# k and v of the first eight units on 128 partitions; five w_out tiles in own memory, decoded among the units

## The chip, the cores and the metric

The program runs on one core of a Trainium2 chip. The metric is the time of one execution in microseconds on the device; a kernel's time is the median of its runs. The kernel before took 1453.11 us (three runs, 1452.28 to 1455.67).

## The reference

q, k, v, p and the output are fp32, and three parts follow one another. `w_in`, `w_out` and the weights of the last part come as 8-byte numbers, so a tile of 128 x 512 is 512 KB.

```
# q, k, v: (8 batches, 8 heads, 576 tokens, 64);  p: (8, 8, 32, 64)
p_packed = sm_attn(p, k, v)            # softmax(p k^T / 8) v : 32 rows per head
out = sm_attn(q, p_packed, p_packed)   # every q row attends to those 32 rows
x = out.transpose(0, 2, 1, 3).reshape(4608, 512)
r = relu(x @ w_in)                     # w_in 512 x 2048
x = (s * r * r + b) @ w_out            # w_out 2048 x 512
y = ((x @ w1) * (x @ w2)) @ w3 @ w_out2   # 512 -> 1024 -> 1024 -> 512
```

A softmax over 576 keys does not care in which order the keys stand, as long as scores, exponentials and the rows of v use the same order.

## The kernel before, in words

A *unit* is half the heads (four) of one batch; there are 16, and `N1 = 8` of them, batches 0 to 3, are worked off in a loop of its own at the start (`for i in range(N1 + OFF)`, line 584, eleven passes, i = 0 to 10). The other eight are planned into the later steps and keep their old form. In the loop several units are under way at once: pass i transposes k of unit i, takes the scores of unit i - 1, transposes the exponentials of unit i - 2 and multiplies unit i - 3 by v.

The steps of a unit, with their names and lines:

- `load_k`, `load_v` (lines 281 and 290): one DMA each, 576 KB, three buffers each. Token `6 p + j` of a head stands on partition `p` of 96, so a partition holds four heads of six tokens of 64 numbers; one run in memory is six tokens, 1536 bytes.
- `A_tr(u, h)` (line 324): head h of k is transposed on TensorE, two tokens' worth of columns (128) at a time, three transposes of 96 columns, and copied out by ScalarE (288 columns). Ahead of them stand multiplications of zeros (`zero`), three for units 0 to 4 and one after, whose result is overwritten.
- `B_s1` (line 341): scores, eight matmuls of 288 columns. The contraction is over 64 rows (one of two parities of token) and four heads stand side by side as 4 x 32 columns of the array. `B_sm1`, `B_sm2`: maximum on DVE, exponential on ScalarE, reciprocal.
- `C_tr(u, hf)` (line 393): two times three transposes of 96 columns of the exponentials, each with one copy by ScalarE.
- `D_mm` (line 406): 6 x 4 matmuls, 96 rows of contraction, 32 x 64 results. `D_ev` transposes the result and stores it in `ppT`.

Between these the loop decodes the 16 tiles of w_in (`decode_win`: a raw 8-byte tile is turned into fp32 by one ScalarE square, lines 141 and 142, and four DVE operations, lines 146 to 165), works on q of batch 0 (`q_step`), and from pass `WS = 6` to 9 multiplies the results of batches 0 and 1 by w_in (`w_pair`). The decoded w_in lies in eight tiles with the tag `sh` (`winx`), and `win_store` writes it to memory for later use. All fp32 matmuls that aren't transposes appear as two records in the trace.

After the loop come 256 steps, 32 for each of eight batches (16 tiles of w_out on each half of the tokens): `step_h` (line 679, six matmuls of 288 columns, then relu and square) runs three steps ahead of `step_x` (line 710, twelve matmuls with one w_out tile, `wo_t[f]`). The first 16 steps need the 16 w_out tiles as they come: `wo_load` fetches a raw tile, `wo_dec` (line 511) decodes it and splits it into two parts (`split`, line 76: ScalarE the upper, DVE the rest). Raw tiles of w_in, w_out and later weights share four buffers (`RAWB`), decoded ones three (`XB`); the later loads of the stored w_in (`W_load`) take these three too. w_out tiles 0 to 7 lie in a pool `wop` that is opened once the unit loop's pools are closed, tiles 8 to 15 take over the eight `sh` tiles.

Order: the lines stand in program order, but the framework moves instructions by its own simulated time, except those pinned by `keep_in_program_order`, among them nearly all loads on SP, the queue that issues all DMAs. Each engine then works strictly in order.

Of the kernel before, what the change touches and what calls it, by code (L numbers as in the profile page):

```python
# [9 lines left out]
F32 = mybir.dt.float32  # L10
F32R = mybir.dt.float32r
# [4 lines left out]
AF = mybir.ActivationFunctionType  # L16
# [6 lines left out]
def fused_kernel(  # L23
# [144 lines left out]
    if True:  # L168
# [97 lines left out]
        def kt_ps(name):  # L266
            return ps0.tile([P, 512], F32, tag="kt", name=name, bufs=2)
# [4 lines left out]
        def m_ps(name):  # L272
            return ps0.tile([P, 512], F32, tag="m", name=name, bufs=2)
# [3 lines left out]
            for n in range(NFC * NPAIR // 2)  # L277
        ]
        kt, vt, kT, S1, E1, E1T, PV = {}, {}, {}, {}, {}, {}, {}

        def load_k(u):
            b, g = divmod(u, NG)
            kt[u] = a1.tile([TP, 4, NJ, D], F32, tag="k", name="k", bufs=3)
            ins = nc.sync.dma_start(
                out=kt[u], in_=k[b, 4 * g:4 * g + 4].rearrange("h (p j) d -> p h j d", j=NJ)
            )
            if u:
                tc.keep_in_program_order(ins)

        def load_v(u):  # L290
            b, g = divmod(u, NG)
            vt[u] = a1.tile([TP, 4, NJ, D], F32, tag="v", name="v", bufs=3)
            ins = nc.sync.dma_start(
                out=vt[u], in_=v[b, 4 * g:4 * g + 4].rearrange("h (p j) d -> p h j d", j=NJ)
            )
            tc.keep_in_program_order(ins)

        pTd, pz = {}, {}
        A = {"p": a1}
# [23 lines left out]

        def A_tr(u, h):

            if h == 0:
                kT[u] = A["p"].tile([P, 4, HS], F32, tag="kT", name="kT", bufs=2 if u < N1 else 1)
            ps = kt_ps("ktp") if u < N1 else a2_ps("ktp")
            src = kt[u][:, h] if u < N1 else kt.pop((u, h))
            if u < N1:  # L330
                for _ in range(3 if u < 5 else 1):
                    nc.tensor.matmul(ps, zero[:, :P], zero, start=True, stop=True)
            for jj in range(HJ):
                nc.tensor.transpose(
                    ps[:, jj * TP:(jj + 1) * TP],
                    src[:, 2 * jj:2 * jj + 2, :].rearrange("p j d -> p (j d)"),
                    ident[:TP, :TP],
                )
            nc.scalar.copy(kT[u][:, h], ps[:, :HS])

        def B_s1(u):
            if u < N1:
                t = ps0.tile([P, 2, 512], F32, tag="s1", name="s1p")
                ps = t[:, 0], t[:, 1], t
            else:
                ps = a2_ps("s1p"), a2_ps("s1p")
            for par in range(2):
                rows = slice(D * par, D * (par + 1))
                for h in range(4):
                    nc.tensor.matmul(  # L350
                        ps[par][NP * h:NP * (h + 1), :HS], pTd[u // 4][rows, u % 4, NP * h:NP * (h + 1)],
                        kT[u][rows, h], start=True, stop=True,
                    )
            S1[u] = ps

        def B_sm1(u):
            ps = S1.pop(u)[2]
            mx = a1.tile([P, 4], F32, tag="mx", name="mx", bufs=3)
            nc.vector.tensor_reduce(out=mx[:, 0:1], in_=ps[:, :, :HS], axis=AX.XY, op=ALU.max)
            nc.vector.tensor_scalar_mul(mx[:, 1:2], mx[:, 0:1], -SC)  # L360
            e = a1.tile([P, 2, HS], F32, tag="E1", name="E1", bufs=2)
            nc.scalar.activation(
                e, ps[:, :, :HS], AF.Exp, bias=mx[:, 1:2], scale=SC, accum_out=mx[:, 2:3]
            )
            E1[u] = (e, mx)

# [24 lines left out]
            rec[u] = r  # L391

        def C_tr(u, hf):
            if hf == 0:
                E1T[u] = A["p"].tile([TP, NJ, P], F32, tag="E1T", name="E1T", bufs=2 if u < N1 else 1)
            ps = m_ps("etp") if u < N1 else a2_ps("etp")
            for jj in range(HJ):
                nc.tensor.transpose(
                    ps[:TP, jj * P:(jj + 1) * P], E1[u][0][:, hf, jj * TP:(jj + 1) * TP], ident
                )  # L400
            dst = E1T[u][:, hf * HJ:(hf + 1) * HJ, :].rearrange("p a b -> p (a b)")
            nc.scalar.copy(dst, ps[:TP, :HJ * P])
# [3 lines left out]
        def D_mm(u):  # L406

            ps = m_ps("pvp") if u < N1 else a2_ps("pvp")  # L410
            for j in range(NJ):
                for h in range(4):
                    nc.tensor.matmul(
                        ps[NP * h:NP * (h + 1), :D], E1T[u][:, j, NP * h:NP * (h + 1)],
                        vt[u][:, h, 2 * (j % HJ) + j // HJ, :], start=j == 0, stop=j == NJ - 1,
                    )
            x = A["p"].tile([P, 2, D], F32, tag="pvx", name="pvx", bufs=2 if u < N1 else 1)
            nc.vector.tensor_tensor(
                out=x, in0=ps[:, None, :D].to_broadcast([P, 2, D]),
                in1=rec.pop(u).to_broadcast([P, 2, D]), op=ALU.mult,  # L420
            )
            PVX[u] = x
# [88 lines left out]
        def wo_dec(f):  # L511
            d = wod.pop(f)
            d.square()
            d.bits1()
            d.bits2()
            if f >= NW // 2:
                wo_t[f] = sh.tile([P, 2, DM], F32R, tag="sh", name=f"wo{f}", bufs=NW // 2)
            else:
                wo_t[f] = wop[0].tile([P, 2, DM], F32R, name=f"wo{f}")
            split(wo_t[f][:, 0, :], wo_t[f][:, 1, :], d.f)  # L520

        NW = NFC * NPAIR
        OFF = 3

        NWARM = 18
        zero = wch_p.tile([P, 2, FC], F32, tag="wpst", name="zero", bufs=4)[:, 0]
# [53 lines left out]
        def w_pair(j):  # L580
            wps = q_ps if j % 2 == 0 else kt_ps
            W_pair(j, [wps("wps") for _ in range(2)])

        for i in range(N1 + OFF):
            jq = i - AS
            if 1 <= i < N1 + 1:
                load_v(i - 1)
            if i < N1:
                A_tr(i, 0)
            if i + 2 < N1:  # L590
                load_k(i + 2)
# [12 lines left out]
            if i >= OFF:  # L604
                D_mm(i - OFF)
            if i < N1:
                A_tr(i, 2)
            decode_win()
            if i < N1:
                A_tr(i, 3)  # L610
# [12 lines left out]
            if WS <= i < WS + 4:  # L623
                w_pair(2 * (i - WS) + 1)
            if 2 <= i < 2 + NTILE:
                load_q(0, i - 2)
            if i == N1:
                for f in range(4):
                    wo_load(f)
            if i > N1:  # L630
                for _ in range(3):
                    win_store()
        ps = ps0.tile([P, 2, 512], F32, tag="s1", name="warm")[:, 0]
        for n in range(8):
            wh = wch[0, 0][0][:, 0]
            tc.keep_in_program_order(nc.tensor.matmul(ps, wh[:, :P], wh, start=True, stop=True))
        ctx0.close()
        ctx1.close()
        wop[0] = ctx_a.enter_context(pool("wop", "right"))
        for f in range(3):  # L640
            wo_load(f + 4)
            wo_dec(f)


        ctx2 = ExitStack()
# [3 lines left out]
        def a2_ps(name):  # L649
            return psh.tile([P, 512], F32, tag="a2", name=name, bufs=2)  # L650
# [305 lines left out]
                      w3T[m, half][:, 1].rearrange("p a b -> p (a b)"), ps, pin=pin)  # L956
        for idx in range(NST):
            n, r = divmod(idx, 2 * FB1)
            if idx + 7 < FB1:
                wo_load(idx + 7)  # L960
            for _ in range(2):
                if stores:
                    win_store()
            if idx + 3 < FB1:
                wo_dec(idx + 3)
            if idx in PPS:
                pp_split(PPS.index(idx) + 1)
            if idx == PPS[2]:
# [423 lines left out]
```

## Time and profile before

| | |
|---|---|
| median of three runs | 1453.11 us |
| the profiled execution | 1454.21 us |
| its span, first to last instruction | 1451.7 us |
| mean granted TensorE clock | 0.992 of full |
| TensorE busy | 1422.3 us, 98% |
| DVE busy | 939.2 us, 65% |
| ScalarE busy | 753.1 us, 52% |
| HBM read, written | 182.98 MB, 44.04 MB |

PE is TensorE, ACT ScalarE, POOL GpSimd; SP issues the DMAs. A matmul's record is longer than the distance to the next, since matmuls overlap; the chain of waits counts only the time up to the next piece, and so shows their pace. The chain follows the work that ended last back from the end, at each step to what released it. The share of DMA is the mean over 16 engines that move the data; a little above 1 means that all were at work all the time.

### The profile page before, as it was taken

The page shows a single profiled execution, that of the slowest core. Times are in us where ns is not written, and L with a number is a line of the kernel's source. Part 1 is how long each engine was busy: PE and PEld are TensorE (multiplying, and loading weights), DVE is VectorE, ACT ScalarE, POOL GpSimd, SP SyncE. Part 2 cuts the span into 40 slices and gives each one's busy share as a digit, 9 for nine tenths or more (in the row PEclk, how much of TensorE's full clock was granted, in tenths as well). Part 3 has the DMA queues.
Part 4 walks back from the last instruction along what each step waited for, and adds up shares of the span by engine and source line. Part 5 has one row for each costly group of instructions (what it writes and reads, how often), then busy time and mean ns, then how long its engine had stood idle before and what let it go on. Part 6 is the DMA issues. An engine that isn't in the chain of part 4 may idle for free.

```text
span 1451.7 us, 28061 instructions
## 1 busy us (share of the span) xinstructions
PE 1422.3 (98%) x10858; PEld 1336.3 (92%) x10858; DVE 939.2 (65%) x1842; ACT 753.1 (52%) x1625; POOL 3.8 (0%) x38
## 2 busy tenths in 40 slices
PE   8999999999999999999999999999999999999997
PEld 5559999999999989999899998999999999999997
DVE  5769644565665776667898637466585756757556
ACT  3567655675656776567876634242243333324323
POOL 0000000000000000000000000000000000000000
PEclk8999999999999999999999999999999999999999
DMA  9967422132263344255563533776675856757551
GB/s 237 245 201 242 140 62 53 44 104 71 90 183 109 114 140 126 64 165 160 177 207 130 175 110 133 227 226 193 189 234 162 253 171 195 227 165 215 160 165 44
DMA packets 179365, 228.86 MB, mean 158 GB/s; under 512 B 55329, under 2 KB 115745, under 8 KB 179233
## 3 DMA queue, kind: packets, MB, share of 16 engines
q1 hardware_dynamic: 179232, 227.07, 53.6%
q8 instruction: 86, 1.41, 0.4%
q14 instruction: 47, 0.38, 0.1%
HBM read 182.98 MB, written 44.04 MB: 156 GB/s over the span
## 4 chain that ended last, share of the span: by engine, by line
PE 90%; ACT 3%; DMA 3%; DVE 2%; issue 1%; SPq 0%; POOL 0%; ACTq 0%; POOLq 0%; DVEq 0%
PE xps L86 9%; PE xps L90 9%; PE xps L89 9%; PE prod L86 7%; PE prod L90 7%; PE prod L89 7%; PE hps L86 5%; PE hps L90 4%; PE hps L89 4%; PE yps L89 4%; PE yps L90 4%; PE yps L86 4%; DMA raw<-in_moe_w_in_dram 2%; PE scp L204 2%; PE s1p L350 1%; PE qtp L190 1%
## 5 line engine op out<-in xcount | busy, mean ns | idle before, releaser
L90 PE MATMUL xps<-gh,wo 128*128 128x288 f32 (+1 forms) x1024 | 302.4, 299 | 0.0
L89 PE MATMUL xps<-gl,wo 128*128 128x288 f32 (+1 forms) x1024 | 302.2, 298 | 0.0
L86 PE MATMUL xps<-gh,wo 128*128 128x288 f32 (+1 forms) x1024 | 291.9, 300 | 1.6 <-DVE wo L81 1.6
L86 PE MATMUL prod<-xc,whl 128*128 128x384 f32 x672 | 226.2, 337 | 2.9 <-ACT Ta L1032 1.8
L90 PE MATMUL prod<-xc,whl 128*128 128x384 f32 x672 | 225.0, 335 | 0.0
L89 PE MATMUL prod<-xc,whl 128*128 128x384 f32 x672 | 224.8, 335 | 0.0
L89 PEld LDWEIGHTS xps<-gl,wo 128*128 128x128 f32 x1024 | 193.2, 189 | 3.0 <-issue 1.4
L90 PEld LDWEIGHTS xps<-gh,wo 128*128 128x128 f32 x1024 | 193.0, 189 | 2.8 <-issue 1.9
L86 PEld LDWEIGHTS xps<-gh,wo 128*128 128x128 f32 x1024 | 188.3, 189 | 5.0 <-POOL gh L695 2.0
L691 ACT ACTIVATE r<-hps 128x288 f32<-128x288 f32 x256 | 104.6, 410 | 134.1 <-PE hps L90 130.4
L703 DVE TENSOR_TENSOR gl<-r,gh 128x288 fp32r<-128x288 f32 x256 | 115.3, 454 | 77.5 <-ACT r L700 74.7
L86 PE MATMUL hps<-ATh,wpl 128*128 128x288 f32 x512 | 153.8, 301 | 5.9 <-ACT r L691 5.0
L1032 ACT COPY Ta<-prod 128x384 f32<-128x384 f32 x96 | 46.1, 480 | 215.4 <-PE prod L90 214.6
L90 PE MATMUL hps<-ATh,wph 128*128 128x288 f32 x512 | 152.8, 298 | 0.0
L89 PE MATMUL hps<-ATl,wph 128*128 128x288 f32 x512 | 152.6, 298 | 0.0
L90 PE MATMUL yps<-w4c,op 128*128 128x256 f32 x504 | 142.2, 282 | 0.0
L89 PE MATMUL yps<-w4c,op 128*128 128x256 f32 x504 | 142.1, 282 | 0.0
L86 PE MATMUL yps<-w4c,op 128*128 128x256 f32 x504 | 140.9, 280 | 0.0
L86 PEld LDWEIGHTS prod<-xc,whl 128*128 128x128 f32 x672 | 126.2, 188 | 7.4 <-ACT Ta L1032 3.8
L89 PEld LDWEIGHTS prod<-xc,whl 128*128 128x128 f32 x672 | 126.2, 188 | 0.0
L90 PEld LDWEIGHTS prod<-xc,whl 128*128 128x128 f32 x672 | 126.1, 188 | 0.0
L700 ACT ACTIVATE r<-r 128x288 f32<-128x288 f32 x256 | 112.7, 444 | 4.7
(158 smaller groups left out, 2582.9 us busy)
## 6 DMA issues: line engine op xcount, KB each, us to landing
whl<-whl SPq DMA_DIRECT2D x336, 256.0 KB, 3.1
raw<-in_moe_w_dram SPq DMA_DIRECT2D x32, 512.0 KB, 4.2
raw<-in_moe_w_out_dram SPq DMA_DIRECT2D x24, 512.0 KB, 4.5
x<-win SPq DMA_DIRECT2D x48, 256.0 KB, 2.8
v<-in_v_dram SPq DMA_DIRECT2D x16, 576.0 KB, 7.7
q<-in_q_dram SPq DMA_DIRECT2D x72, 128.0 KB, 4.4
x<-xst SPq DMA_DIRECT2D x16, 576.0 KB, 3.2
out_dram<-O SPq DMA_DIRECT2D x72, 128.0 KB, 2.4
```

The source lines that it names most:

```text
L86: ins = nc.tensor.matmul(ps, wl, xh, start=start, stop=False, **kw)
L89: nc.tensor.matmul(ps, wh, xl, start=False, stop=False, **kw)
L90: nc.tensor.matmul(ps, wh, xh, start=False, stop=stop, **kw)
L190: nc.tensor.transpose(ps[:, pr * P:pr * P + n], src[:n, 2 * pr:2 * pr + 2, :].rearrange("p h d -> p (h d)"), ident[:n, :n],)
L204: nc.tensor.matmul(ps[sl, c:c + 64], qT[b, t][:, pr, sl], ppT[:, b // 2, pr, b % 2, :], start=True, stop=True,)
L350: nc.tensor.matmul(ps[par][NP * h:NP * (h + 1), :HS], pTd[u // 4][rows, u % 4, NP * h:NP * (h + 1)], kT[u][rows, h], start=True, stop=True,)
L691: nc.scalar.activation(r, ps[:, :HS], AF.Relu)
L700: nc.scalar.activation(r, r, AF.Square)
L703: nc.vector.tensor_tensor(out=gl[:, :HS], in0=r, in1=gh[:, :HS].bitcast(F32), op=ALU.subtract)
L1032: tc.keep_in_program_order(nc.scalar.copy(out, src))
```

## The change

Units 0 to 7 hold their k and v differently. Two heads lie on one another on 128 partitions, 64 each, with nine tokens on a partition (one run of memory: 2304 bytes); a unit takes two DMAs for k and two for v. `A_tr` is called three times a unit instead of four, each with three transposes of 128 columns and one copy of 384; the zero matmuls ahead of them are three for units 0 to 2, two for units 3 and 4, none after. The scores are eight matmuls again, of 320 and 256 columns, laid side by side so that their 576 columns are contiguous. `C_tr` becomes 18 matmuls of 64 columns against the identity instead of six transposes, `D_mm` 36 matmuls of 64 rows instead of 24 of 96.

w_out tiles 0 to 4 get a pool of their own (`wop0`) that is there from the start; tiles 5 to 12 take over the `sh` tiles and 13 to 15 a pool opened after the loop. The first four are loaded at pass 5 and decoded at passes 7 to 10, where tiles 4 to 7 are loaded; all 16 `win_store` are issued at passes 6 to 9, four in each. After the loop tile 4 is decoded, and the steps decode five tiles ahead (`AHEAD`) where it was three, and load nine ahead where it was seven. The diff, without the parts that keep the old form for the later units:

```diff
+        J2, JE = S // 64, (S // 64 + 1) // 2
         def load_k(u):
-            kt[u] = a1.tile([TP, 4, NJ, D], F32, tag="k", name="k", bufs=3)
-            ins = nc.sync.dma_start(
-                out=kt[u], in_=k[b, 4 * g:4 * g + 4].rearrange("h (p j) d -> p h j d", j=NJ)
-            )
+            kt[u] = a1.tile([P, 2 * J2, D], F32, tag="k", name="k", bufs=3)
+            for a in range(2):
+                h0 = 4 * g + 2 * a
+                ins = nc.sync.dma_start(
+                    out=kt[u][:, a * J2:(a + 1) * J2].rearrange("p j d -> p (j d)"),
+                    in_=k[b, h0:h0 + 2].rearrange("h (p j) d -> (h p) (j d)", j=J2),
+                )
...
         def A_tr(u, h):
+            if u < N1:
+                if h == 0:
+                    kT[u] = a1.tile([P, J2, P], F32, tag="kT", name="kT", bufs=2)
+                ps = kt_ps("ktp")
+                for _ in range(3 if u < 3 else 2 if u < 5 else 0):
+                    nc.tensor.matmul(ps, zero[:, :P], zero, start=True, stop=True)
+                for c in range(3):
+                    j = 2 * (3 * h + c)
+                    nc.tensor.transpose(
+                        ps[:, c * P:(c + 1) * P],
+                        kt[u][:, j:j + 2, :].rearrange("p j d -> p (j d)"), ident,
+                    )
+                nc.scalar.copy(
+                    kT[u][:, 3 * h:3 * h + 3].rearrange("p a c -> p (a c)"), ps[:, :3 * P]
+                )
+                return
...
         def B_s1(u):
+            for odd_, h in ((o, h) for o in range(2) for h in range(4) if u < N1):
+                n = JE if odd_ == 0 else J2 - JE
+                s0, par = divmod(J2 * (h // 2) + odd_, 2)
+                rows = slice(D * par, D * (par + 1))
+                c0 = 512 - 64 * JE if odd_ == 0 else 0
+                nc.tensor.matmul(
+                    ps[odd_][NP * h:NP * (h + 1), c0:c0 + 64 * n],
+                    pTd[u // 4][rows, u % 4, NP * h:NP * (h + 1)],
+                    kT[u][rows, s0:s0 + n, 64 * (h % 2):64 * (h % 2 + 1)], start=True, stop=True,
+                )
...
         def C_tr(u, hf):
+            if u < N1:
...
+                for j in range(j0, j1):
+                    e0 = 64 * (j // 2 + (JE if j % 2 else 0))
+                    for r in range(2):
+                        nc.tensor.matmul(
+                            ps[64 * r:64 * (r + 1), 64 * (j - j0):64 * (j - j0 + 1)],
+                            E1[u][0][:, e0:e0 + 64],
+                            ident.rearrange("p (a r n) -> p r a n", r=2, n=NP)[:, r],
+                            start=True, stop=True,
+                        )
...
         def D_mm(u):
+            for j in range(J2 if u < N1 else 0):
+                for h in range(4):
+                    rows = slice(64 * (h % 2), 64 * (h % 2 + 1))
+                    nc.tensor.matmul(
+                        ps[NP * h:NP * (h + 1), :D], E1T[u][rows, j, h // 2, :],
+                        vt[u][rows, h // 2, j, :], start=j == 0, stop=j == J2 - 1,
+                    )
...
         def wo_dec(f):
-            if f >= NW // 2:
+            if WOA <= f < WOA + NW // 2:
                 wo_t[f] = sh.tile([P, 2, DM], F32R, tag="sh", name=f"wo{f}", bufs=NW // 2)
             else:
-                wo_t[f] = wop[0].tile([P, 2, DM], F32R, name=f"wo{f}")
+                wo_t[f] = wop[f >= WOA].tile([P, 2, DM], F32R, name=f"wo{f}")
-        OFF = 3
+        OFF, WOA, AHEAD = 3, 5, 5
+        wop[0] = ctx_a.enter_context(pool("wop0", "right"))
...
             if WS <= i < WS + 4:
                 w_pair(2 * (i - WS) + 1)
+                for _ in range(4):
+                    win_store()
-            if i == N1:
+            if i == WS - 1:
                 for f in range(4):
                     wo_load(f)
-            if i > N1:
-                for _ in range(3):
-                    win_store()
+            if i >= N1 - 1:
+                wo_dec(i - N1 + 1)
+                wo_load(i - N1 + 5)
...
-        wop[0] = ctx_a.enter_context(pool("wop", "right"))
-        for f in range(3):
+        wop[1] = ctx_a.enter_context(pool("wop1", "right"))
+        for f in range(4, AHEAD):
+            wo_dec(f)
             wo_load(f + 4)
-            wo_dec(f)
...
-            if idx + 7 < FB1:
-                wo_load(idx + 7)
-            for _ in range(2):
-                if stores:
-                    win_store()
-            if idx + 3 < FB1:
-                wo_dec(idx + 3)
+            if idx + AHEAD < FB1:
+                wo_dec(idx + AHEAD)
+            if idx + AHEAD + 4 < FB1:
+                wo_load(idx + AHEAD + 4)
```

## Rows read from the trace of the kernel before

**Rows 1.** The page: busy us, share of the span, instructions, of TensorE.

```profile
PE 1422.3 (98%) x10858; PEld 1336.3 (92%) x10858; DVE 939.2 (65%) x1842; ACT 753.1 (52%) x1625; POOL 3.8 (0%) x38
```

**Rows 2.** Busy us by stretch: engines, then TensorE clock, DMA share, GB/s.

```profile
10.00:30.00 20.00, 14.43 (x65) 8.71 (x66) 12.02 (x24) 6.59 (x15) 0.00 (x0) 0.66 1.02 262
...
50.00:68.70 18.70, 16.46 (x220) 10.57 (x220) 12.04 (x33) 9.78 (x25) 0.00 (x0) 1.00 1.09 242
68.70:103.30 34.60, 34.15 (x370) 15.74 (x367) 23.55 (x61) 23.42 (x56) 0.42 (x8) 1.00 0.81 232
103.30:159.20 55.90, 52.23 (x394) 49.94 (x394) 53.20 (x117) 43.66 (x102) 2.70 (x24) 0.97 0.66 201
159.20:840.00 680.80, 676.03 (x5660) 643.74 (x5660) 442.11 (x1067) 450.22 (x1058) 0.00 (x0) 1.00 0.40 120
```

**Rows 3.** Chain of waits, 60 to 104 us: start, us, what (x records).

```profile
53.15 13.27 DMA raw<-in_moe_w_in_dram
...
70.15 0.46 PE etp L398 x3
70.61 0.24 PE ktp L332
...
72.61 0.47 PE pvp L413 x24
...
78.15 0.62 PE scp L204 x16
...
101.89 1.85 PE warm L636 x8
```

**Rows 4.** Waits of TensorE, 103.3 to 159.2 us: total, times, longest us.

```profile
PE hps L86 <- ACT r L691: 2.0, 1, 2.0
PE xps L86 <- DVE wo L81: 1.6, 2, 1.0
```

**Rows 5.** Chain of waits, 103 to 160 us.

```profile
143.35 0.60 DVE x L152
...
146.46 0.34 DVE x L146
...
147.13 0.61 DVE wo L81
147.76 3.09 DMA x<-win
150.87 0.62 ACT sh L78
...
155.99 0.24 PE xps L89
156.23 0.14 PE xps L90
```

**Rows 6.** DMA of 22:26, 82:86, 1044:1048 us; counts under each size are cumulative.

```profile
DMA packets 577, 1.01 MB, mean 254 GB/s; under 512 B 28, under 2 KB 510, under 8 KB 577
...
q1 hardware_dynamic: 577, 1.01, 102.8%
...
DMA packets 403, 1.44 MB, mean 360 GB/s; under 512 B 47, under 2 KB 56, under 8 KB 402
...
q1 hardware_dynamic: 402, 1.43, 102.5%
...
DMA packets 741, 1.36 MB, mean 340 GB/s; under 512 B 78, under 2 KB 78, under 8 KB 741
...
q1 hardware_dynamic: 741, 1.36, 94.4%
```

**Rows 7.** Groups of TensorE, 0 to 110 us: busy us, mean ns, idle before.

```profile
L413 PE MATMUL pvp<-v,E1T 96*32 96x64 f32 x384 | 11.3, 224 | 0.0
```

**Rows 8.** Timeline of SP: start, us, what.

```profile
76.69 0.32 SPq L293 DMA_DIRECT2D v<-in_v_dram  x1
```

**Rows 9.** Waits of DVE, 66 to 103 us: total, times, longest us.

```profile
DVE x L146 <- DMA raw<-in_moe_w_out_dram: 3.5, 1, 3.5
```

More of the change, by code (lines that the diff above doesn't have):

```diff
@@ L279, in fused_kernel @@
         kt, vt, kT, S1, E1, E1T, PV = {}, {}, {}, {}, {}, {}, {}
+        J2, JE = S // 64, (S // 64 + 1) // 2
         def load_k(u):
             b, g = divmod(u, NG)
-            kt[u] = a1.tile([TP, 4, NJ, D], F32, tag="k", name="k", bufs=3)
-            ins = nc.sync.dma_start(
-                out=kt[u], in_=k[b, 4 * g:4 * g + 4].rearrange("h (p j) d -> p h j d", j=NJ)
-            )
+            kt[u] = a1.tile([P, 2 * J2, D], F32, tag="k", name="k", bufs=3)
[5 more added lines that the diff above has]
+                )
+                if u or a:
+                    tc.keep_in_program_order(ins)
             if u:
@@ L291, in load_v @@
             b, g = divmod(u, NG)
[L292 to L296, printed above, removed]
+            vt[u] = a1.tile([P, 2, J2, D], F32, tag="v", name="v", bufs=3)
+            for a in range(2):
+                h0 = 4 * g + 2 * a
+                ins = nc.sync.dma_start(
+                    out=vt[u][:, a].rearrange("p j d -> p (j d)"),
+                    in_=v[b, h0:h0 + 2].rearrange("h (p j) d -> (h p) (j d)", j=J2),
+                )
+                tc.keep_in_program_order(ins)
         pTd, pz = {}, {}
@@ L324, in A_tr @@
         def A_tr(u, h):
-            if h == 0:
[L327 to L332, printed above, removed]
+            if u < N1:
[14 more added lines that the diff above has]
+                return
+            if h == 0:
+                kT[u] = A["p"].tile([P, 4, HS], F32, tag="kT", name="kT", bufs=1)
+            ps = a2_ps("ktp")
+            src = kt.pop((u, h))
             for jj in range(HJ):
@@ L346, in B_s1 @@
                 ps = a2_ps("s1p"), a2_ps("s1p")
-            for par in range(2):
+            for odd_, h in ((o, h) for o in range(2) for h in range(4) if u < N1):
[8 more added lines that the diff above has]
+                )
+            for par in range(0 if u < N1 else 2):
                 rows = slice(D * par, D * (par + 1))
@@ L356, in B_sm1 @@
         def B_sm1(u):
-            ps = S1.pop(u)[2]
+            ps = S1.pop(u)[2].rearrange("p a c -> p (a c)")[:, 512 - 64 * JE:512 + 64 * (J2 - JE)]
             mx = a1.tile([P, 4], F32, tag="mx", name="mx", bufs=3)
-            nc.vector.tensor_reduce(out=mx[:, 0:1], in_=ps[:, :, :HS], axis=AX.XY, op=ALU.max)
+            nc.vector.tensor_reduce(out=mx[:, 0:1], in_=ps, axis=AX.X, op=ALU.max)
             nc.vector.tensor_scalar_mul(mx[:, 1:2], mx[:, 0:1], -SC)
-            e = a1.tile([P, 2, HS], F32, tag="E1", name="E1", bufs=2)
+            e = a1.tile([P, S], F32, tag="E1", name="E1", bufs=2)
             nc.scalar.activation(
-                e, ps[:, :, :HS], AF.Exp, bias=mx[:, 1:2], scale=SC, accum_out=mx[:, 2:3]
+                e, ps, AF.Exp, bias=mx[:, 1:2], scale=SC, accum_out=mx[:, 2:3]
             )
@@ L393, in C_tr @@
         def C_tr(u, hf):
+            if u < N1:
+                if hf == 0:
+                    E1T[u] = a1.tile([P, J2, 2, NP], F32, tag="E1T", name="E1T", bufs=2)
+                ps = m_ps("etp")
+                j0, j1 = (0, JE) if hf == 0 else (JE, J2)
+                for j in range(j0, j1):
[7 more added lines that the diff above has]
+                        )
+                nc.scalar.copy(
+                    E1T[u][:, j0:j1].rearrange("p j a n -> p (j a n)"), ps[:, :64 * (j1 - j0)]
+                )
+                return
             if hf == 0:
-                E1T[u] = A["p"].tile([TP, NJ, P], F32, tag="E1T", name="E1T", bufs=2 if u < N1 else 1)
-            ps = m_ps("etp") if u < N1 else a2_ps("etp")
+                E1T[u] = A["p"].tile([TP, NJ, P], F32, tag="E1T", name="E1T", bufs=1)
+            ps = a2_ps("etp")
             for jj in range(HJ):
@@ L410, in D_mm @@
             ps = m_ps("pvp") if u < N1 else a2_ps("pvp")
-            for j in range(NJ):
+            for j in range(J2 if u < N1 else 0):
[4 more added lines that the diff above has]
+                        vt[u][rows, h // 2, j, :], start=j == 0, stop=j == J2 - 1,
+                    )
+            for j in range(0 if u < N1 else NJ):
                 for h in range(4):
@@ L608, in fused_kernel @@
             decode_win()
-            if i < N1:
-                A_tr(i, 3)
             if i >= OFF:
```

## The prediction

> **What bounds the kernel now.** I read the page's busy shares first: TensorE is busy 98% of the span [rows 1], so the loss, if any, is local. The table by stage says where [rows 2]. From 159.2 us on TensorE is busy 676.0 of 680.8 us at the full clock, DVE only 442: nothing that the change touches bounds that part, and a microsecond won before it comes through whole, as one lost does. Three stages lie ahead of it.
>
> Up to about 67 us the transfers bound: their share is 1.02 to 1.09, while TensorE is busy 16.5 of 18.7 us in the last part. The chain of waits agrees: 13.3 us on a w_in tile issued at 53.15, ScalarE's square of it at 66.5, and only then unbroken TensorE [rows 3]. From there to 101.9 us the chain is TensorE alone, and from 103.3 to 159.2 us the first 16 steps of w_out run with DVE at 53.2 of 55.9 us. TensorE's waits there are 2.0 us on ScalarE and 1.6 us on a w_out tile [rows 4]. The chain shows the cause of the 2.0 us: a load of the stored w_in at 147.76, for which ScalarE's in-order split waited until 150.87; after that pause of TensorE 14 of its pieces, the last at 155.99, took 0.24 us where those behind them take 0.14 [rows 5]: the clock had fallen to its lower level (1.2 GHz). That costs 14 x 0.10 = 1.4 us. So the third stage loses 2.0 + 1.6 + 1.4 = 5.0 us.
>
> **Part 1: k and v on 128 partitions.** A load was 384 runs of 1536 bytes (96 partitions, four heads); it becomes 256 runs of 2304 bytes in two transfers. What does a run cost? Between 22 and 26 us, 1.028 x 16 engines x 4 us = 65.8 us of engine time went into 482 runs of 1536 bytes, 67 of 4 KB and a few small ones; between 82 and 86 us, 65.6 us into 346 runs of 4 KB, so 190 ns each; that leaves (65.8 - 12.7)/482 = 110 ns for 1536 bytes. Between 1044 and 1048 us, 60.4 us went into 663 runs of 2 KB on 128 partitions: 91 ns [rows 6]. So 1536-byte runs move at 14 GB/s an engine, the wider ones at 22. For 2304 bytes three estimates: by the 2 KB rate 91 x 2304/2048 = 102 ns; on the line from 1536 bytes to 4 KB 110 + 768/2560 x 80 = 134; at the 1536-byte rate 165. I take 118, between the two lower ones. A load then takes (384 x 110 - 256 x 118)/16 = 0.75 us less of all 16 engines (1.0 to 0). Eleven of them (k of units 0 to 6, v of 0 to 3) stand ahead of that w_in tile: 8.3 us (11 to 0). I count 7, because before 40 us TensorE's own chain with the zero matmuls sets the pace. The sixteen extra issues cost 0.3 to 0.5 us each on SP, which mostly waits there; hidden, since transfers are queued some 10 us deep.
>
> Next in line after that tile is TensorE, and there the change adds. D_mm goes from 24 matmuls to 36, each recorded twice (384 records in eight units [rows 7]); 24 records take 0.47 us [rows 3], so 48 records 0.94 and 72 records 1.41 us: +0.47 us a unit if the pace is set per record, about 0 if the two row halves run side by side. C_tr goes from six transposes (two of 0.46 us) to 18 matmuls of 64 columns, the form of q_sc, whose 16 records (eight matmuls) take 0.62 us [rows 3]: 18/8 x 0.62 = 1.40, +0.48 us. Nothing shown lets these be cheaper than 0. A_tr keeps about 1 us of transposes (twelve of 96 columns, now nine of 128) and loses its last zero matmul per group from unit 5 on, 0.24 us each [rows 3]. After 67 us some 4.5 D_mm, 4 C_tr and six zero matmuls lie: 2.1 + 1.9 - 1.5 = +2.5 us (-1.5 to +4). Scores keep their 576 columns, the maximum its 576 elements; evictions get shorter by about 0.3 us a unit on ScalarE, which is no bound.
>
> On D_mm a figure can be weighed. 24 records in 0.47 us are 19.6 ns each [rows 3]. The Trainium skill, TensorE: Matmul & The Clock Gate (Wait — 56ns, not 53.3ns?), has starts never closer than about 25 ns. By that the 24 added records would cost 0.60 us, 0.6 us more over 4.5 units; the row is already below that floor, so the row's figure stands.
>
> **Part 2: five w_out tiles in own memory.** Four are decoded inside the unit loop, all 16 stores of w_in and eight w_out loads are issued there. A decode is on DVE 0.34 + 3 x 0.60 + 0.61 = 2.75 us [rows 5], on ScalarE some 1.3. The trace already decodes three tiles, without the last step, before 103 us; now it is four whole ones and perhaps three partly: up to 11 us more DVE in a stage where it is busy 23.6 of 34.6 us [rows 2]. It fits, barely. For friction on TensorE I put 1.5 us (0 to 11). In the third stage DVE then has 11 us less to do in 55.9, so the 1.6 us on w_out tiles go. The late w_in load waits for a buffer that w_out decodes hold, so I expect two thirds of the 3.4 us around it to go too: -1.6 - 2.3 = -4 us (0 to -5). What is late next there is TensorE itself.
>
> SP is in order. Ahead of v of units 5 to 7 now stand four w_out loads, eight stores and one load that waits for a raw buffer, that is for DVE's third decode operation on the first tile. The last v, issued at 76.7 us [rows 8], will be issued later relative to the units, behind about 4 x 1.5 + 8 x 0.7 = 12 us of transfers; its D_mm runs some 24 us after that issue, so I cost this at nothing; without that cover it is the rest of the transfer, up to 5 us.
>
> Sum: -7 + 2.5 + 1.5 - 4 = -7. The profiled execution took 1454.2 us, 1.1 above the median of the runs, 1453.1; off the median the forecast is 1446.1.
>
> **Rivals.**
> *The rows save nothing.* Runs cost by the byte (165 ns). For it: reads of k and v share HBM with everything else, and no 2304-byte run is in this trace. Against: 2 KB runs are cheaper than 1536-byte ones [rows 6]. Then 0 + 2.5 + 1.5 - 4 = 0: 1453. The Trainium skill, DMA: Bandwidth & Descriptors (Specifications), puts the least transfer for line rate at 512 bytes; by that rule 1536 bytes are already enough and this rival holds. The trace speaks against it: the wider runs move at one and a half times the rate.
>
> *In-order waits on w_out (the slower side).* Four decodes are put into DVE's and ScalarE's order among the evictions on which TensorE waits, while their transfers stand behind k, v and the stores. The trace has one such wait, 3.5 us on DVE [rows 9], hidden by TensorE's backlog. If three tiles wait so with DVE full, 11 us: -7 + 2.5 + 11 - 4 = +2.5, and a TensorE pause of that length took the clock down in the third stage, another 1.4 us: +4, 1457. It decides from 8.5 us of waiting on.
>
> *The clock falls.* The zero matmuls of units 5 to 7 are gone. From 10 to 30 us, after a long wait, the mean clock was 0.66; from 50 us, with one zero matmul per group, it stayed at 1.00 [rows 2]. If TensorE waits for k at unit 5 and runs one unit's work (6 us) at the lower level, +6: 1452.
>
> *More than forecast.* Runs at 102 ns all count (-11), the row halves overlap (0), friction 0.5, third stage -5: about -14 with the zero matmuls, 1439.
>
> **How the numbers follow.** Forecast 46%, own range 1442 to 1450; no saving by rows 20%; waits on w_out 16%; more 10%; clock 8%. A measurement of this kernel cannot tell less than about 0.2%, 2.9 us. Faster by more than that: 42 of the first, all of the larger gain, a quarter of the first rival, 3 of the clock's: 60%. Slower: most of the waits' case and a little of the first rival and the clock's, 18%. Within: 22%. The range 1437 to 1456 leaves out most of the slower case above and a little below.
>
> **What would show it.** k and v loads as 256 runs, the last w_in tile decoded near 60 us; if it stays at 66, part 1's saving is wrong. D_mm at 1.4 and C_tr at 1.4 us a unit. The first steps begin at about 100 us with five or more w_out tiles ready; the sixteenth ends near 152 us instead of 159, with no TensorE wait on w_out and no stretch at half clock. Waits of DVE or ScalarE on w_out transfers of over 8 us before 100 us, or a clock under 1 between 50 and 70 us, would make it wrong.

## The result and the profile after

The changed kernel took 1439.58 us (median of four runs, 1435.08 to 1440.33) against 1453.14 us before (four runs): 13.6 us less by the medians. The ratio, here and below, is formed from the means of the runs: 0.9897 [0.9874, 0.9921], 15 us less where 7 were forecast. The profiled execution took 1439.51 us, its span is 1437.7 us.

The page, TensorE's line, answers to [rows 1]: TensorE has 375 records more and is busy 10.6 us less.

```profile
PE 1411.7 (98%) x11233; PEld 1333.9 (93%) x11233; DVE 938.6 (65%) x1842; ACT 750.8 (52%) x1617; POOL 3.6 (0%) x38
```

Busy time by stretch of the changed kernel (columns as in [rows 2]):

```profile
10.00:30.00 20.00, 17.38 (x214) 12.27 (x213) 17.14 (x38) 11.59 (x25) 0.00 (x0) 0.91 0.92 327
30.00:50.00 20.00, 16.95 (x359) 12.19 (x357) 19.76 (x51) 13.09 (x31) 0.00 (x0) 1.00 1.06 349
50.00:60.00 10.00, 10.00 (x128) 6.12 (x127) 6.41 (x20) 4.97 (x11) 0.10 (x1) 0.66 1.01 281
60.00:93.20 33.20, 32.81 (x550) 17.56 (x549) 30.12 (x71) 24.61 (x54) 0.28 (x7) 1.00 0.86 308
93.20:143.00 49.80, 49.80 (x396) 48.57 (x395) 44.95 (x101) 39.22 (x94) 2.54 (x24) 1.00 0.62 177
```

Up to 50 us the engines of the DMA are about as busy as before (0.92 and 1.06) and move 327 to 349 GB/s where it was 242 to 262 [rows 2]. From 93.2 to 143 us TensorE never idles. And there is something new: from 50 to 60 us the clock is 0.66.

The chain of waits of the changed kernel, in order of time (start, us, what):

```profile
31.63 0.67 ACT m L142
32.30 0.05 issue
...
36.80 1.14 PE pvp L464 x72
...
43.97 1.02 PE pvp L464 x62
...
47.72 0.61 PE etp L434 x15
48.33 1.65 issue
49.98 0.22 PE etp L434
...
54.25 1.86 PE pvp L464 x62
56.11 0.83 PE ktp L343 x3
56.94 1.18 PE wps L534 x4
...
85.01 0.58 PE etp L434 x20
85.59 0.26 PE ppp L484
85.85 0.62 PE etp L434 x16
...
88.18 0.46 PE pvp L464 x20
...
91.27 1.86 PE warm L694 x8
93.13 0.13 PE hps L86
```

Three things are to be seen. From 32.36 to 90.58 us the chain is TensorE alone, with the one pause below. Before, transfers stood in it until the square of the last w_in tile (its chain of waits):

```profile
66.50 0.70 ACT m L142
```

The first `wps` (the first product of `w_pair`) starts at 56.94 us here. D_mm's 72 records take 1.14 us in one block, C_tr's 36 take 0.58 + 0.62. And in the middle of a C_tr TensorE stands still for 1.65 us with no releaser ("issue"); behind that pause 62 records of the next D_mm take 1.86 us where 62 took 1.02 ahead of it: the lower level of the clock, 1.2 GHz.

So the difference to before splits in four stretches. The ends are the first `wps`, the first `hps`, the second store of `xst` and the end of the span, taken from the timelines; the columns behind `after` are kernels of the experiments below.

| stretch, change in us against before | forecast | after | after_again | fewer_rec | p1_only | p2_two |
|---|---|---|---|---|---|---|
| start to the first `wps` (before 68.21) | -7 | -11.3 | -14.7 | -14.8 | -11.8 | -4.3 |
| to the first `hps` (35.37) | +4 | +0.7 | +0.7 | +0.4 | +2.4 | -1.9 |
| to the second store (99.06) | -4 | -6.8 | -6.8 | -6.8 | +0.2 | -5.8 |
| to the end (1249.06) | 0 | +3.4 | +2.0 | +2.3 | +1.0 | +2.3 |
| sum (span 1451.7) | -7 | -14.0 | -18.8 | -18.9 | -8.3 | -9.7 |

Each column is one profiled execution.

### The profile page after: what moved, and what is told of

It reads as the page before. It is cut to its first block, busy times and chain, and to the rows that moved or that the text cites. A ratio compares the mean times of both kernels' runs of the same rounds, so it can differ in the third digit from the quotient of the medians.

```text
span 1437.7 us, 28804 instructions
## 1 busy us (share of the span) xinstructions
PE 1411.7 (98%) x11233; PEld 1333.9 (93%) x11233; DVE 938.6 (65%) x1842; ACT 750.8 (52%) x1617; POOL 3.6 (0%) x38
## 3 DMA queue, kind: packets, MB, share of 16 engines
q8 instruction: 89, 1.46, 0.4%
## 4 chain that ended last, share of the span: by engine, by line
PE 90%; ACT 3%; DMA 3%; DVE 2%; issue 1%; SPq 1%; ACTq 0%; DVEq 0%
PE xps L86 9%; PE xps L89 9%; PE xps L90 9%; PE prod L86 7%; PE prod L90 7%; PE prod L89 7%; PE hps L86 5%; PE hps L89 4%; PE hps L90 4%; PE yps L89 4%; PE yps L90 4%; PE yps L86 4%; PE scp L204 2%; PE qtp L190 1%; PE wps L534 1%
## 5 line engine op out<-in xcount | busy, mean ns | idle before, releaser
L90 PE MATMUL xps<-gh,wo 128*128 128x288 f32 (+1 forms) x1024 | 301.7, 299 | 0.0
L86 PE MATMUL xps<-gh,wo 128*128 128x288 f32 (+1 forms) x1024 | 286.1, 299 | 0.0
```

Of the source, the lines that this page charges most:

```text
L86: ins = nc.tensor.matmul(ps, wl, xh, start=start, stop=False, **kw)
L90: nc.tensor.matmul(ps, wh, xh, start=False, stop=stop, **kw)
```

## The experiments

**The parts alone: p1_only and p2_two.** First the new form of k and v with the old handling of w_out, then the other way round with two w_out tiles in own memory, since the old k and v leave no room for five.

```diff
-        OFF, WOA, AHEAD = 3, 5, 5     # p1_only: w_out, stores and loads as before
+        OFF = 3
...
-        OFF = 3                        # p2_two: from the kernel before
+        OFF, WOA, AHEAD = 3, 2, 5
```

> Part 1 alone: k and v on 128 partitions, the w_out tiles loaded, stored and decoded as before. Theory A (transfers): the loads free the front by some 14 us and this is most of the gain; the unit loop ends near 92 us as in the changed kernel, the sixteenth w_out step follows after 50 to 55 us as before, and the time is 1441 to 1446 (8 to 12 us of the 14). Theory B (decoding): the earlier decoding gives most, so part 1 alone gives at most 5 us: 1448 or more.

> Part 2 alone, with k and v as before; two w_out tiles in own memory instead of five, since no more fits beside the old k and v, and tiles 2 to 9 take over the w_in tiles. Theory A: the front does not move, so that the w_in tile is decoded at 66 us still and eight w_out loads and 16 stores now stand among the k and v loads; the third stage gains up to 7 us and the front loses some: 1447 to 1453. Theory B: 7 us or more are gained: 1446 or less.

p1_only: 1445.57 us, ratio 0.9936 [0.9913, 0.9959], so 9.3 us. p2_two: 1449.37 us, 0.9962 [0.9944, 0.9981], 5.5 us. They add up to the 15 us of the whole, within their intervals. p2_two's twelve runs lie wide, 1443.74 to 1456.09, and its profile is of the fastest. In p1_only the first `wps` starts at 56.37 instead of 68.21, and the third stage is as it was, 99.22 us long, with the waits of [rows 4] in it. TensorE's waits in p1_only (engine, line, us, times, longest):

```profile
PE hps L86 <- ACT r L746: 2.0, 1, 2.0
PE xps L86 <- DVE wo L81: 1.6, 2, 1.0
```

In the changed kernel both are gone, and so is the half clock there: 1.00 from 93.2 to 143 us. That p2_two's front would not move was expected and is not what its profile shows: its first `wps` starts at 63.92, 4.3 us earlier than before, with the old k and v. Whether that belongs to part 2 or to this fast execution is not shown.

**Partitions or length of runs: split_runs and forms.** split_runs cuts each k and v load of the changed kernel in two by columns, so that the runs are 1280 and 1024 bytes, still on 128 partitions.

```diff
+                for c0, c1 in ((0, JE), (JE, J2)):
+                    ins = nc.sync.dma_start(
+                        out=kt[u][:, a * J2 + c0:a * J2 + c1]...,
+                        in_=k[b, h0:h0 + 2]...[:, c0 * D:c1 * D],
+                    )
```

> The changed kernel with each k and v transfer cut in two by columns: on 128 partitions still, but runs of 1280 and 1024 bytes (512 a load instead of 256). Theory L (the length of a run makes it cheap): runs at 90 to 110 ns give 2.9 to 3.5 us a load, worse than before's 2.6, the front's 14 us are lost and the time is 1450 or more. Theory P (the partitions make it cheap): bytes per us stay, the time is within 4 us of the changed kernel's 1439.6.

1442.92 us, ratio 0.9918 [0.9894, 0.9942]: with runs shorter than those of the kernel before, 12 of the 15 us stay; the first `wps` starts at 57.55, 10.7 us earlier than before.

forms holds nothing but loads of k and v, 1.18 MB each, six per form; nothing of the reference is computed.

```diff
+    FORMS = ((96, 384), (128, 384), (96, 768), (128, 768), (128, 576), (128, 256))   # partitions, fp32 of a run
...
+                src = src.rearrange("(a p c) -> p a c", p=np_, c=run)
```

> Transfers alone, nothing of the reference is computed: six loads of 1.18 MB (one batch of k, then of v) in each of six forms, 96 or 128 partitions by runs of 1536 and 3072 bytes, and 128 partitions by 2304 and 1024 bytes, at most four under way. Theory L: at one length 96 and 128 partitions take the same, and 3072 bytes move at least 1.3 times as fast as 1536. Theory P: 96 partitions move at some 220 GB/s whatever the length, 128 partitions at 340 GB/s or more, also with 1536 bytes.

DVE copies a column as each load lands. The timeline of DVE (start, us, operation), 1536-byte runs on 96 and then on 128 partitions:

```profile
24.67 0.15 DVE L70 COPY acc<-f96x 96x1 f32<-96x1 f32 x1 [5.18 <-DMA f96x<-in_k_dram]
30.00 0.15 DVE L70 COPY acc<-f96x 96x1 f32<-96x1 f32 x1 [5.19 <-DMA f96x<-in_k_dram]
35.11 0.15 DVE L70 COPY acc<-f96x 96x1 f32<-96x1 f32 x1 [4.96 <-DMA f96x<-in_k_dram]
...
50.67 0.15 DVE L70 COPY acc<-f128x 128x1 f32<-128x1 f32 x1 [3.07 <-DMA f128x<-in_k_dram]
53.85 0.15 DVE L70 COPY acc<-f128x 128x1 f32<-128x1 f32 x1 [3.02 <-DMA f128x<-in_k_dram]
56.95 0.15 DVE L70 COPY acc<-f128x 128x1 f32<-128x1 f32 x1 [2.95 <-DMA f128x<-in_k_dram]
```

One load every 5.2 us against one every 3.1 us, with the same runs. The other distances: 4.9 us for 96 x 3072 bytes, 2.95 for 128 x 3072, 3.03 for 128 x 2304, 3.4 for 128 x 1024. And by stretch, inside the first two forms (length, then busy us of DVE and POOL, clock, DMA share, GB/s):

```profile
22.00:35.00 13.00, 0.30 (x2) 0.00 (x0) 1.00 1.01 204
50.00:57.00 7.00, 0.36 (x3) 0.00 (x0) 1.00 0.93 325
```

In both the engines are busy nearly all the time; one run of 1536 bytes holds an engine for 1.01 x 16 / (204000/1536) = 122 ns on 96 partitions and for 0.93 x 16 / (325000/1536) = 70 ns on 128. The number of partitions decides, by a factor of 1.7; the length of a run is worth some 15% between 1024 and 3072 bytes. The Trainium skill, SBUF — State Buffer (Door 1: The DMA port swizzle), says that transfer rate depends on how many ports the partitions reach, and that partitions 0 to 63 reach only one half of the ports. 96 partitions reach them all, but two thirds of the partitions go through that half; an estimate from this page is 0.75 of the full rate. The runs here agree in direction and show 0.60 (3.1 us a load against 5.2).

**The zero matmuls and the eight after the loop: after_again, zero1, zero0, nowarm.** The changed kernel once more; with one zero matmul per group of units 5 to 7; with none at all; and without the eight `warm` matmuls behind the loop.

```diff
-                for _ in range(3 if u < 3 else 2 if u < 5 else 0):
+                for _ in range(3 if u < 3 else 2 if u < 5 else 1):   # zero1
+                for _ in range(0):                                    # zero0
...
-        for n in range(8):
+        for n in range(0):                                            # nowarm
```

> The changed kernel once more, as the measure for the other kernels of this call: 1435 to 1441. Theory C (clock): runs with a granted clock of 0.997 are some 4 us faster than those with 0.995, since in those the stretch at the lower level after 50 us is missing.

> The changed kernel with one zero matmul per transposition group for units 5 to 7 instead of none (nine of 0.24 us more). Theory C (the lower clock from 50 to 56 us comes because TensorE has too little to do at units 5 and 6): the clock stays at 1.00, 3 us come back, 1 to 2 us go to the zeros: 1 to 3 us below the changed kernel. Theory I (it comes from the pause of 1.65 us for which no releaser is shown): the fall stays and the time is the same or 1 to 2 us longer.

> The changed kernel without any zero matmul ahead of the transposes. If the zeros hold the clock, the granted clock is near 0.6 for most of the time between 10 and 55 us, units take twice as long and the time is 4 to 15 us above the changed kernel. If the transfers alone bound up to 55 us, nothing is lost, and the time is within 2 us or up to 3 us shorter.

> The changed kernel without the eight matmuls (1.86 us on the chain at 91.3 us) between the unit loop and the steps. If TensorE goes straight on to the first step: 1.5 to 2 us shorter. If what the step needs is not ready, or the pause takes the clock down: the same or up to 3 us longer.

after_again 1438.67 us, 0.9893 [0.9871, 0.9915]; zero1 1439.25, 0.9902 [0.9881, 0.9922]; nowarm 1438.64, 0.9895 [0.9874, 0.9916]; zero0 1448.61, 0.9973 [0.996, 0.9987]. So the zero matmuls as a whole hold the clock (zero0 is at 0.67 from 30 to 50 us) and are worth 10 us. Those of units 5 to 7, which the change took away, are worth nothing that shows. The eight behind the loop bring no gain that shows: nowarm's first `hps` starts at 88.49 instead of 89.60 us, but its second store at 182.00 instead of 181.84.

after_again's use lies in its profile. The same program ran in 1434.69 us there, and the pause at the same record is shorter. Its timeline (start, us, operation, idle before), and the stretch behind the pause in after and in after_again:

```profile
48.00 0.68 PE L434 MATMUL etp<-ident,E 128*64 128x64 f32 x15
49.31 0.22 PE L434 MATMUL etp<-ident,E 128*64 128x64 f32 x1 [0.64 <-issue]
```

```profile
50.00:56.00 6.00, 6.00 (x95) 4.24 (x94) 2.92 (x10) 3.12 (x7) 0.00 (x0) 0.54 1.09 295
```

```profile
50.00:56.00 6.00, 6.00 (x121) 3.83 (x119) 5.55 (x19) 4.61 (x10) 0.10 (x1) 1.00 1.08 272
```

With 0.64 us of pause the clock stayed at 1.00, with 1.65 us it fell to a mean of 0.54, and the first `wps` started at 53.55 us in the one and at 56.87 in the other. Of the ten runs of the two, three took 1434.7 to 1435.1 us and seven 1438.3 to 1441.3. That the fall separates these two groups, as expected, is not shown: over the whole run the mean clock is 0.996 to 0.997 in the three and 0.995 to 0.998 in the seven, and zero1's profile holds 1.00 there and took 1439.73 us.

**Why TensorE pauses: shift26, shift64, shift100.** In five kernels (after, after_again, nowarm, zero1, p1_only) the pause stood behind TensorE's 601st or 602nd matmul record, 0.6 to 1.65 us long, and ended 2.4 to 2.7 us behind a packet of 16 KB in a DMA queue whose kind is "instruction" (89 such packets, 1.46 MB, in the whole run). 22466 instructions of TensorE, a load of weights for each matmul, over 89 packets make 252, so about 126 matmul records, a packet. If TensorE waits for its instructions, the pause must follow the count of records and not the place in the program. Three kernels put small matmuls of zeros at the start:

```diff
+        for n in range(26):          # 64, 100
+            nc.tensor.matmul(ps[:, :64], zero[:, :P], zero[:, :64], start=True, stop=True)
-        for n in range(NWARM):
+        for n in range(NWARM - 3):   # 8, 12
             nc.tensor.matmul(ps, zero[:, :P], zero, start=True, stop=True)
```

> The changed kernel with 26 small matmuls of zeros (64 columns) put ahead of everything, in place of three of the eighteen large ones; nothing else differs. In five kernels TensorE paused for 0.64 to 1.65 us in the middle of C_tr near 50 us with no releaser, each time behind its 601st or 602nd matmul record and 2.4 to 2.7 us behind the packet of 16 KB in its instruction queue. Theory I (TensorE ran out of instructions and waits for the next block): the pause moves 26 records earlier, to the middle of the 16 score matmuls s1p (behind about the 6th), and ends 2.4 to 2.7 us behind that packet. Theory J (the pause belongs to this place of the program: the exponentials or a psum buffer of C_tr): it stays ahead of the 16th etp record. The time: 1434.5 to 1435.5 us where the clock stays, 1438 to 1441 where it falls.

> As the last one with 64 small matmuls in place of eight large ones. Theory I: the pause lies 64 records earlier, within the 62 records of D_mm behind about the 57th of them, some 2 us earlier in time. Theory J: unchanged place. If the block is asked for earlier in relation to what TensorE still has to do, the pause gets shorter, and under 0.6 us the clock should stay: then near 1435.

> As the last two with 100 small matmuls in place of twelve large ones. Theory I: the pause lies 100 records earlier, behind about the 21st of the 62 records of D_mm near 44.5 us, where the records follow one another at 16 ns, so the block before it is eaten fast; pause 0.6 to 2 us, or none if the packet comes before. Theory J: unchanged place. The time between 1434 and 1441 by whether the clock falls.

As times they failed: 1444.87, 1452.12 and 1453.11 us (ratios 0.9951 [0.9934, 0.9968], 0.9997 [0.9983, 1.001], 1.0001 [0.9985, 1.0016]). A matmul of 64 columns of these zeros took 0.21 us, so the start was late: shift64's first transpose came at 19.31 us. In the place of the pause they decide. Timeline of shift64, then its packet, then the records up to the pause (columns as in [rows 2]):

```profile
54.33 0.33 PE L434 MATMUL etp<-ident,E 128*64 128x64 f32 x2
56.02 0.69 PE L434 MATMUL etp<-ident,E 128*64 128x64 f32 x17 [1.36 <-issue]
```

```profile
q8 instruction: 1, 0.02, 68.4%
```

```profile
0.00:55.90 55.90, 51.25 (x603) 40.20 (x604) 39.77 (x98) 25.90 (x54) 0.70 (x6) 1.00 0.86 287
```

The packet lies between 53.3 and 53.4 us. shift26, in the same way (its packet lies between 65.3 and 65.4 us):

```profile
65.13 0.28 PE L434 MATMUL etp<-ident,E 128*64 128x64 f32 x3
67.87 0.69 PE L434 MATMUL etp<-ident,E 128*64 128x64 f32 x17 [2.46 <-issue]
```

```profile
0.00:67.80 67.80, 56.78 (x729) 41.32 (x730) 48.06 (x122) 31.76 (x68) 0.80 (x7) 0.92 0.87 287
```

shift64 pauses behind record 603, at another place of the program (the third record of a C_tr, where it was the sixteenth of its second half). shift26 doesn't pause at 601, as I had expected, but at 729 = 601 + 128, one block later; shift100 doesn't pause at all. In shift64 and shift26 the pause ends 2.5 to 2.7 us behind the packet. What moves with the count and keeps its distance to the packet is a wait for instructions; the rival, one place in the program, falls. All seven pauses lie inside a C_tr, but at its third, fourth, fourteenth or sixteenth record, and zero1 has one more, 0.49 us at record 729 and 2.6 us behind its packet (56.97), that lies outside, although the profile names something that ended it:

```profile
59.59 1.08 PE L534 MATMUL wps<-winx,ppT 128*64 128x512 f32 x4 [0.49 <-PE etp L434]
```

The Trainium skill, Runtime: NRT & Kernel Launch (Instruction fetch mechanics), says that an engine's instructions come in blocks of 16 KB, 256 instructions, through a DMA queue of its own, and that crossing a block is mostly hidden. The trace agrees on the block (252 instructions a packet); here, with the share of the DMA above 1, it was not hidden.

**Moving the boundaries: fewer_rec and more_rec.** In after_again's timeline the 128 records ahead of the pause last 4.8 us and the blocks of 128 before and behind these 6.4 and 7.5 us, because D_mm's come 14 ns apart and the zero matmuls 230 ns or more. fewer_rec takes 19 records away at the start, by a few plain fp32 matmuls of two records each in place of more fp32r ones; more_rec adds 92.

```diff
-        for n in range(NWARM):
-            nc.tensor.matmul(ps, zero[:, :P], zero, start=True, stop=True)
+        for n in range(4):                                   # fewer_rec; zero4 is zero as fp32
+            nc.tensor.matmul(ps, zero4[:, :P], zero4, start=True, stop=True)
...
+        for n in range(104):                                 # more_rec; zb is zero as bf16
+            nc.tensor.matmul(ps[:, :32], zb[:, :P], zb[:, :32], start=True, stop=True)
+        for n in range(NWARM - 12):
+            nc.tensor.matmul(ps, zero[:, :P], zero, start=True, stop=True)
...
+                if u < 3:                                    # fewer_rec, in A_tr
+                    nc.tensor.matmul(ps[:, :3 * P], zero4[:, :P], zero4[:, :3 * P], start=True, stop=True)
```

> The changed kernel with 19 matmul records fewer at the start: four plain fp32 matmuls of zeros (two records each, 4 passes) in place of 18 fp32r ones, and one of 384 columns in place of the three zero matmuls ahead of each group of units 0 to 2; the columns' time stays about the same. Theory I (TensorE runs out of instructions: a block of 128 records is asked for when the one before it is used up and takes some 6.5 us under full transfers): the boundaries lie 19 records later in the program, where 128 records last 6.3 to 7 us by the trace of the changed kernel instead of 4.7, so the pause near 50 us shrinks under 0.4 us and the clock stays at 1.00 in every run: median 1434.5 to 1436 against 1438.7. Theory J (the pause belongs to this place of the program, or is given by the saturated transfers of k and v): pause of 0.6 us or more and 1438 to 1441 as before. If the clock at the start suffers from the changed zero matmuls, that is seen before 30 us and costs 1 to 4 us.

> The changed kernel with 104 small bf16 matmuls of zeros (32 columns) and 6 large ones at the start in place of 18 large ones, so 92 records more. Theory I: the boundaries lie 92 records earlier in the program (36 later by the count modulo 128), where 128 records last 6.6 to 7.5 us: no pause over 0.5 us near 50 us, clock at 1.00: 1434.5 to 1436, plus what the start is later by, if the small ones take longer than the twelve large ones (at most 2 us). Theory J: pause of 0.6 us or more in the same place of the program, 1438 to 1441.

fewer_rec took 1433.81 us (1433.17 to 1434.61), ratio 0.9869 [0.9854, 0.9884]: faster than before and, run for run, than all ten runs of the changed kernel, the nearest of them by 0.1 us. The two were not run side by side, and the intervals of their ratios overlap. No pause without a releaser is left before 300 us, and the clock holds (columns as in [rows 2]):

```profile
10.00:30.00 20.00, 15.20 (x207) 9.82 (x206) 16.28 (x37) 11.64 (x25) 0.00 (x0) 1.00 0.89 316
30.00:50.00 20.00, 18.12 (x374) 13.11 (x373) 19.68 (x48) 13.20 (x32) 0.00 (x0) 1.00 1.06 347
50.00:60.00 10.00, 9.95 (x146) 4.84 (x144) 8.76 (x27) 6.07 (x14) 0.10 (x1) 1.00 1.00 272
```

It also holds at 1.00 from 10 to 30 us, where the changed kernel has 0.91; that is worth little, since its first `wps` starts at 53.40 us and after_again's, with 0.91 there, at 53.55. more_rec loses the pause too (1.00 from 45 to 90 us) but took 1436.78 us (1434.4 to 1438.24), 0.9888 [0.9867, 0.991]: its first `wps` starts at 52.46 us, its first `hps` only at 91.31. These 2 us of the unit loop I have not explained. So the pause goes with fewer records ahead of it and with more: by these two kernels what counts is where a block of instructions ends, not how many there are.

## Why the prediction was right in direction and wrong in size

**k and v, the step that failed.** "What does a run cost?": I read 110 ns for 1536 bytes against 91 ns for 2 KB and 80 ns per further 2560 bytes [rows 6] as a price of the run's length, took 118 ns for 2304 bytes from it, and put -0.75 us a load. Those rows differ in the number of partitions as well, and that is what they show: alone, the same run takes 122 ns on 96 partitions and 70 ns on 128. The old load was priced rightly, 2.62 us (half of 5.25; 384 runs of 110 ns on 16 engines make 2.64). The new one took 1.51 us (half of 3.03), so 95 ns a run and not 118. That is -1.11 a load, and eleven of them -12.2 us where I had 8.3 and counted 7.

What arrived at the first `wps` is -14.7 us without the half clock, -11.3 with it and -11.8 in p1_only. That 12.2 lies among these is in part luck. In after and after_again the transfers no longer set that time: from 32.36 and 32.62 us on their chains are TensorE alone up to it, where I had put that before 40 us only. And -4.3 us stand in p2_two's profile, without the new k and v. From 10 to 30 us the clock rose from 0.66 to 0.91 too. These parts are not taken apart.

**The sum.** In the profile of after the front brought 4.3 us more than forecast, the unit loop behind it 3.3 and the third stage 2.8, and 3.4 were lost again at the end. So the front is the largest of the terms that were off, and what it was added up from, the price of a run, the one that can be named.

**The first rival** (a run costs by the byte, nothing saved) falls with it: 327 to 349 GB/s. **More than forecast**, the rival with a chance of 10%, gave the time that was measured, 1439; its 102 ns a run, the rate of the 2 KB rows on 128 partitions, lay nearest to the 95 measured, and its front (-11) came near. That the total agrees is luck: its -14 left out the loss behind the second store and took the third stage at -5.

**TensorE's additions.** Forecast +2.5 us and 1.5 us of friction, measured +0.7 from the first `wps` to the first `hps`. The additions were nearly right, and p1_only, which has them without the decodes, shows +2.4. Worked out from the starts of all records between the two marks, four units' D_mm went from 5.0 to 6.7 us and their C_tr from 3.3 to 4.8, so +0.42 and +0.38 us a unit where +0.47 and +0.48 were forecast, and the zero matmuls gave back 1.6 (forecast 1.5). Unforecast are the scores, 3.7 to 2.2 us. The friction of the decodes doesn't show, with DVE busy 30.12 of 33.2 us: p2_two, which has the decodes without the additions, is 1.9 us shorter there. Why is open.

D_mm was forecast at 1.41 us a unit, three times the 0.47 of 24 records, and took 1.14 in one block. Twenty records of 96 rows take as long before (chain of waits, below) as twenty of 64 rows now (at 88.18 above):

```profile
35.72 0.46 PE pvp L413 x20
```

From start to start the 24 records of 96 rows that begin at 72.61 us lie 14.0 ns apart on average, and the 72 of 64 rows that begin at 36.80 us too. So 23 distances make 0.32 of the 0.47 us and 71 make 0.99 of the 1.14; the other 0.15 us, from the last record to the next piece, come once a block, and the forecast had them three times. The pace per record is the same for both forms. Cut up among other work, as between the two marks, a unit's D_mm took 1.25 us before and 1.68 now.

**The third stage.** Right in kind, -6.8 instead of -4. I had kept a third of the 3.4 us around the late w_in load; all of it went, with the waits on w_out. That makes 5.0 of the 6.8 us, the sum that the prediction found lost there; the other 1.8 are open.

**The clock.** The rival put a fall at unit 5 on the missing zero matmuls. A fall came at that time, behind the pause of 1.65 us. The missing zero matmuls alone don't bring it: after_again, nowarm and fewer_rec lack them too and hold 1.00 there. zero1 has them, pauses 0.83 us, holds 1.00 and takes no less time, 1439.25 us. Whether they would hold the clock behind a pause of 1.65 us is not shown. The pause is TensorE running out of instructions. Before, the same engine used 128 records in 10 to 13 us there; now it uses them in 4.8, and the transfers that it waits behind are still saturated. In the profile of after, against after_again, the pause ended 0.7 us later, and behind it, at the half clock, another 2.6 us were lost up to the first `wps`.

**The waits on w_out** (the slower side) did not come: from 93 to 143 us the view of TensorE's waits is empty.

**A microsecond won early does not come through whole**, though the prediction said so. Behind the second store 2.0 to 3.4 us are given back, 1.0 in p1_only. In after_again TensorE's listed waits behind 185 us sum to 8.1 us where before has 6.6, most of them on ScalarE's `r` and on `wpl`. Why the later steps wait more is open.

## What to carry to other kernels

Count the partitions of a transfer before its bytes: a layout on all 128 partitions was worth 1.7 times the rate of one on 96. When a rate is read from rows that differ in two things, name both as possible causes, or find a row that holds one of them. And when a bound is lifted, look at what is fetched beside the data: many short matmuls under saturated transfers used up their instructions faster than these came, and moving the end of a block of instructions, by 19 records fewer or 92 more at the start, took the pause away.

## What the runs showed of the hardware

- 1.18 MB in runs of 1536 bytes landed every 5.2 us on 96 partitions and every 3.1 us on 128; with 3072 bytes it was 4.9 and 2.95 us (forms).
- TensorE's instructions come in packets of 16 KB, one for about 126 to 128 matmul records, in a DMA queue of the kind "instruction". In seven profiles a pause of 0.64 to 2.46 us ended 2.4 to 2.7 us behind such a packet, at record 601 to 603 or at 729.
- Pauses of 0.64, 0.83 (zero1), 1.06 (p1_only), 1.19 (nowarm) and 1.36 us (shift64) left the granted clock at 1.00 behind them. The one of 1.65 us was followed by 0.54 from 50 to 56 us, and the one of 2.46 us (shift26) by this stretch (columns as in [rows 2]):

```profile
68.90:72.30 3.40, 3.40 (x24) 1.38 (x22) 0.82 (x2) 1.29 (x4) 0.00 (x0) 0.50 0.85 310
```

- Small matmuls laid side by side in the array, four heads of 32 columns, started 14.0 ns apart on average, with 96 rows as with 64 (D_mm before and after).
- Matmuls of fp32r zeros with 64 columns started 0.21 us apart at the start (26 in 5.6 us, shift26); bf16 ones with 32 columns 27 ns (more_rec).
